# First block of a retention and two-MoE kernel: fourteen weight subtractions and five scalings from VectorE to GpSimd, three state scalings from ScalarE to VectorE

## The chip, the cores and the metric

The kernel runs on 1 core of one Trainium2 chip. The metric is device time in microseconds (us) for one execution; the text uses the median of several runs, and one more execution was profiled. The engines named are PE (TensorE: matrix products; PEld is its weight load), DVE (VectorE), ACT (ScalarE), POOL (GpSimd) and SP (SyncE, which here only issues DMAs). Each engine works through its own instructions strictly in their order; semaphores make it wait for the others.

## The reference

```python
# retention, per batch (4) and head (8), 768 steps, head size 64
state = gamma * state + outer(k[t], v[t]);  y[t] = scale * q[t] @ state
x = y as 3072 tokens x 512
# first feed-forward
h = x @ w_in                 # 512 -> 2048
g = maximum(0.01 * h, h)
x = g @ w_out                # 2048 -> 512
# then a mixture of 8 experts, top 1, 512 -> 1024 -> 512, scaled by two gates
```

The change touches the retention and the weights `w_in` and `w_out` of the first feed-forward. These two arrays come in as 64-bit floats.

## The kernel before

The 3072 tokens are worked through in 8 blocks of 384 (`TB`), and a block is 3 chunks of 128 tokens. A chunk is one step of the retention, which is done chunk by chunk: chunks 0 to 2 make block 0, and while block i goes through the feed-forward, the three chunks of block i+1 are computed between its products. Behind the 8 blocks lie routing and the experts, which the change doesn't touch.

**The loop of a block.** Each block runs 16 steps, f = 0 to 15, over 128 of the 2048 hidden columns each. Step f has `mm1` (12 matmuls of 128x384, line L307), then `act` and `act_b`, and `mm2` of the step before (9 matmuls of 128x512, L348), which adds to the three output banks. Every operand is split into a high part, which TensorE multiplies quickly, and a low part, which is the rest; a product is low times high, high times low and high times high. So behind `mm1` comes a chain: ACT scales h by 0.01 (`t`, L325), DVE takes the maximum (`t`, L326), ACT rounds to the high part (`gh`, L328), DVE subtracts for the low part (`gl`, L335). `mm2` begins with `gl`.

**Preparing the weights.** Block 0 also has to bring the 64-bit weights into high and low parts, one piece of 128x512 of `w_in` and one of `w_out` (index 0 and 1) per step. `conv` does it with the letters A and D (ACT, L151 and L157), B and C (DVE, L159 and L164), H (ACT, L176: high part) and L (L178: low part = value minus high part). In step f of block 0 the DVE's order is: `t`, L of the next `w_in` piece, `gl`, L of the next `w_out` piece, then B twice and C twice for the pieces after. `mm2` of step f uses the low part of `w_out` piece f one to two steps after it was made. The raw pieces are loaded by SP through a ring of four pairs of buffers; a load waits until L has read the pair that it overwrites. The constant `LOP` lists the pieces whose L goes to GpSimd; it is empty before.

**The retention chunk.** In step f = 3, 7 and 11 of block 0 the scores of chunks 3, 4 and 5 are made (`attn_a`, PE L229), and DVE multiplies them by a mask (`am`, L235, twice 128x512). In steps 5, 9 and 13 follows `attn_b`: the outputs `y` (L263, L265), the update of the state `U` (L244), the high and low parts of x (`xh` ACT L274, `xl` DVE L275), then `attn_state` (the state bank is copied to SBUF with a scale for each head, tile `sbd`), `attn_q` and `attn_k` (q and k are scaled in place by tables, L213 and L219). The first set of these three, for chunk 3, stands in step 1. Chunks from 6 on have their q and k scaled by GpSimd and their state by VectorE already.

The line that chooses the engine of L is in `conv_op`; n is the piece, x is 0 for `w_in` and 1 for `w_out`:

```python
(nc.gpsimd if (n, x) in LOP else nc.vector).tensor_sub(lo, val, hi.bitcast(F32))
```

Of the kernel before, what the change touches and what calls it, by code (L numbers as in the profile page):

```python
# [14 lines left out]
ACTF = mybir.ActivationFunctionType  # L15
# [17 lines left out]
FS = [1, 0, 2, 0, 0, 1]  # L33
NSLOT = 2 * NP + NS
XW = 516
LOP = ()
LOWV = ()
AHEAD_S = [(p, c) for p in range(2) for c in range(4)]
AHEAD_P = [(p, 2 * g + c) for g in range(2) for p in range(2) for c in range(2)]
# [18 lines left out]
def tile_retention_moe_moe(  # L58
# [12 lines left out]
    nc = tc.nc  # L71
# [12 lines left out]
    kd = mq[:, :48].rearrange("p (c g) -> p c g", c=6)  # L84
    sc = mq[:, 48:72].rearrange("p (c j) -> p c j", c=6)
    past = mq[:, 72:200]
    qd = mq[:, 200:712]
# [50 lines left out]
    def conv_op(o, n, m, x, f):  # L138
# [27 lines left out]
        if o in "HL":  # L166
# [10 lines left out]
            else:  # L177
                (nc.gpsimd if (n, x) in LOP else nc.vector).tensor_sub(lo, val, hi.bitcast(F32))  # L178

# [7 lines left out]
    sbd = [const.tile([128, 4, 128], F32, name="sbd")]  # L187
    n_b = [0]
    U = {}
# [20 lines left out]

    def attn_q(n):
        q = loads[n][0]
        (nc.vector if n in (0, 2, 3, 4, 5) else nc.gpsimd).tensor_mul(q, q, qd)  # L213

    def attn_k(n):
        cc = n % (2 * NC)
        if cc < 5:
            k = loads[n][2].rearrange("p (g d) -> p g d", d=64)
            (nc.vector if n in (2, 3, 4) else nc.gpsimd).tensor_mul(k, k, kd[:, cc].unsqueeze(2).to_broadcast([128, 8, 64]))  # L219

    def pairs():
        return [(j, h, slice(64 * h, 64 * h + 64), slice(j * 128 + 64 * h, j * 128 + 64 * h + 64), slice(j * 128, (j + 1) * 128))
# [23 lines left out]
    def attn_state(n):  # L246

        b, cc = divmod(n, 2 * NC)
        for h in range(2):
            r = slice(64 * h, 64 * h + 64)  # L250
            if 2 < n < 6:
                for j in range(4):
                    nc.scalar.activation(out=sbd[0][r, j, r], in_=U[b][r, j, r], func=ACTF.Copy, scale=sc[r, cc, j:j + 1])
                continue
            nc.vector.tensor_mul(sbd[n % 2 if n < 3 else 0][r, :, r], U[b][r, :, r], sc[r, cc].unsqueeze(2).to_broadcast([64, 4, 64]))

    def attn_y(n, am, tag="m0"):
# [27 lines left out]
    def attn_b(n, am):  # L285
        y = attn_y(n, am)
        if n % 6 < 5:
            attn_U(n)
        attn_x(n, y)
        if n % 6 < 5:  # L290
            attn_state(n + 1)
        attn_next(n)
        if n + 1 < NB * NC:
            attn_q(n + 1)
            attn_k(n + 1)
# [430 lines left out]
    for x in ORDER:  # L726
        k = sum(y[0] == x for y in items)
# [302 lines left out]
    with tc.manual_schedule():  # L1030
# [20 lines left out]
        def keep_warm(n):  # L1051
            for _ in range(n):
                nc.tensor.matmul(warm[:, :256], sbd[0][:, 0], sbd[0].rearrange("p j c -> p (j c)")[:, :256], start=True, stop=True)

        attn_k(0)
        attn_q(1)
        attn_k(1)
        banks = attn_scores(0, ("m0", "m1"))
        keep_warm(KW[0])
# [6 lines left out]
        banks = attn_scores(1, ("x20", "x21"))  # L1066
        keep_warm(KW[2])
        attn_state(1)
        conv("L", -1)

# [6 lines left out]
        attn_next(0)  # L1077
        y = attn_y(1, am1, "x20")
        attn_state(2)
        attn_q(2)  # L1080
        banks = attn_scores(2, ("x22", "h1"))
        keep_warm(KW[3])
# [175 lines left out]
```

## Time and profile before

| | |
|---|---|
| median of 3 runs | 1012.31 us (1010.25 to 1012.48) |
| profiled execution | 1009.34 us, its span 1007.5 us |
| PE busy | 981.7 us (97%) |
| DVE busy | 561.5 us (56%) |
| ACT busy | 447.1 us (44%) |
| POOL busy | 196.4 us (19%) |
| mean granted TensorE clock | 0.995 |

The span is the time from the first to the last instruction in the trace. The shares are means over very different stages: the preparing of weights lies between about 26 and 107 us, the blocks without it follow up to about 650 us, the experts come last. Granted clock 1.00 is TensorE's higher level of 2.4 GHz, 0.50 the lower of 1.2 GHz.

### The profile page before, as it was taken

The page shows a single profiled execution, that of the slowest core. Times are in us where ns is not written, and L with a number is a line of the kernel's source. Part 1 is how long each engine was busy: PE and PEld are TensorE (multiplying, and loading weights), DVE is VectorE, ACT ScalarE, POOL GpSimd, SP SyncE. Part 2 cuts the span into 40 slices and gives each one's busy share as a digit, 9 for nine tenths or more (in the row PEclk, how much of TensorE's full clock was granted, in tenths as well). Part 3 has the DMA queues.
Part 4 walks back from the last instruction along what each step waited for, and adds up shares of the span by engine and source line. Part 5 has one row for each costly group of instructions (what it writes and reads, how often), then busy time and mean ns, then how long its engine had stood idle before and what let it go on. Part 6 is the DMA issues. An engine that isn't in the chain of part 4 may idle for free.

```text
span 1007.5 us, 16953 instructions
## 1 busy us (share of the span) xinstructions
PE 981.7 (97%) x6525; PEld 870.8 (86%) x6525; DVE 561.5 (56%) x1087; ACT 447.1 (44%) x791; POOL 196.4 (19%) x148
## 2 busy tenths in 40 slices
PE   7899999999999999999999999999999999999996
PEld 5787888888889888988989898888888988888995
DVE  5899543534344444443444367465648657666762
ACT  3888332223222222232222233435548667665752
POOL 2001021021012011011110001623323333333122
PEclk9999999999999999999999999999999999999998
DMA  9674222322322222214303004002139779776511
GB/s 365 228 236 150 83 58 59 89 59 58 90 59 58 60 78 69 59 51 98 58 32 74 17 32 168 21 33 75 42 122 310 265 250 318 277 247 216 191 43 35
DMA packets 75366, 121.64 MB, mean 121 GB/s; under 512 B 36238, under 2 KB 36622, under 8 KB 72464
## 3 DMA queue, kind: packets, MB, share of 16 engines
q1 hardware_dynamic: 70352, 105.96, 34.1%
q0 software_dynamic: 4640, 14.18, 4.1%
q8 instruction: 53, 0.87, 0.4%
q10 hardware_dynamic: 288, 0.36, 0.2%
q14 instruction: 33, 0.27, 0.1%
HBM read 125.97 MB, written 13.64 MB: 139 GB/s over the span
## 4 chain that ended last, share of the span: by engine, by line
PE 85%; DVE 7%; ACT 3%; issue 2%; DMA 1%; POOL 1%; another core or an unknown queue 0%; SPq 0%; POOLq 0%; DVEq 0%
PE x L348 24%; PE h L307 24%; PE m L847 10%; PE m L872 10%; PE m L897 3%; PE m L925 3%; PE ay L229 2%; PE y L265 2%; PE y L263 2%; PE xt L816 1%; DVE raw L159 1%; DMA kv<-in_qkv_dram 1%; DVE wl L178 1%; PE u L244 1%; PE lg L476 1%
## 5 line engine op out<-in xcount | busy, mean ns | idle before, releaser
L783 DVE TENSOR_TENSOR wu<-raw,wu 128x1024 fp32r<-128x1024 f32 x114 | 148.9, 1337 | 58.8 <-ACT wu L782 56.5
L326 DVE TENSOR_TENSOR t<-t,h 128x384 f32<-128x384 f32 x127 | 70.1, 552 | 134.6 <-ACT t L325 134.5
L847 PE MATMUL m<-xe,wu 128*128 128x256 f32 x1056 | 137.5, 284 | 0.8 <-DVE gl L859 0.8
L782 ACT CAST wu<-raw 128x1024 fp32r<-128x1024 f32 x136 | 137.2, 1048 | 1.6 <-DMA raw<-in_w_dram 1.4
L325 ACT ACTIVATE t<-h 128x384 f32<-128x384 f32 x127 | 62.2, 490 | 169.7 <-PE h L307 139.9
L847 PEld LDWEIGHTS m<-xe,wu 128*128 128x128 f32 x1056 | 132.4, 191 | 3.7 <-DVE gl L859 1.0
L335 DVE TENSOR_TENSOR gl<-t,gh 128x384 fp32r<-128x384 f32 x127 | 80.5, 634 | 90.9 <-ACT gh L328 90.9
L328 ACT CAST gh<-t 128x384 fp32r<-128x384 f32 x127 | 65.3, 514 | 128.8 <-PE x L348 68.7
L348 PE MATMUL x<-wh,gl 128*128 128x512 f32 x288 | 116.1, 403 | 6.2 <-DVE gl L335 6.2
L348 PE MATMUL x<-wl,gh 128*128 128x512 f32 x288 | 113.9, 395 | 0.0
L348 PE MATMUL x<-wh,gh 128*128 128x512 f32 x288 | 113.5, 394 | 0.0
L872 PE MATMUL m<-wu,gh 128*128 128x512 f32 x352 | 109.1, 391 | 0.0
L455 POOL TENSOR_TENSOR xr<-xr,b 128x512 f32<-128x512 f32 x18 | 21.0, 1165 | 405.0 <-DVE gl L335 241.0
L307 PE MATMUL h<-xh,wl 128*128 128x384 f32 x384 | 85.3, 343 | 0.0
L307 PE MATMUL h<-xl,wh 128*128 128x384 f32 x384 | 82.6, 336 | 0.0
L783 POOL TENSOR_TENSOR wu<-raw,wu 128x1024 fp32r<-128x1024 f32 x22 | 55.5, 2531 | 137.8 <-ACT wu L782 131.0
L307 PE MATMUL h<-xh,wh 128*128 128x384 f32 x384 | 82.1, 334 | 0.0
L872 PEld LDWEIGHTS m<-wu,gh 128*128 128x128 f32 x352 | 66.3, 188 | 12.5
L348 PEld LDWEIGHTS x<-wh,gl 128*128 128x128 f32 x288 | 54.3, 189 | 21.3 <-DVE gl L335 8.8
L872 PE MATMUL m<-wu,gl 128*128 128x512 f32 x176 | 69.8, 396 | 1.2 <-DVE gl L859 0.9
L307 PEld LDWEIGHTS h<-xh,wl 128*128 128x128 f32 x384 | 67.1, 188 | 3.8
L307 PEld LDWEIGHTS h<-xl,wh 128*128 128x128 f32 x384 | 69.0, 188 | 0.0
(232 smaller groups left out, 1519.8 us busy)
## 6 DMA issues: line engine op xcount, KB each, us to landing
raw<-in_w_dram SPq DMA_DIRECT2D x175, 512.0 KB
kv<-in_qkv_dram SPq DMA_DIRECT2D x22, 1024.0 KB
x2d<-xr SPq DMA_DIRECT2D x24, 256.0 KB
kv<-in_qkv_dram SPq DMA_DIRECT2D x4, 512.0 KB
t<-b SPq DMA_TRANSPOSE x36
stg<-in_w_dram SPq DMA_DIRECT2D x1, 512.0 KB
kv<-x2d,gidx POOLq DMA_INDIRECT x18
mq<-in_cm_dram ACTq DMA_DIRECT2D x1, 256.0 KB
```

The source lines that it names most:

```text
L307: nc.tensor.matmul(h, wcols(a, fc * 512 + k * 128, 128), x[:, k, :], start=(n == 0), stop=(n == 11))
L325: nc.scalar.activation(out=t, in_=h, func=ACTF.Copy, scale=0.01)
L326: nc.vector.tensor_max(g, t, h)
L328: nc.scalar.copy(out=ghi, in_=g)
L335: nc.vector.tensor_sub(glo, g, ghi.bitcast(F32))
L348: nc.tensor.matmul(x2ps[i][t], a[:, ts], wcols(w, f % 4 * 512), start=(f == 0 and n == 0), stop=(f == 15 and n == 2))
L782: nc.scalar.copy(out=hi, in_=src)
L783: (nc.gpsimd if g == 0 or (p, c) in POOL_LO[g >= NP] else nc.vector).tensor_sub(lo, src, hi.bitcast(F32))
L847: nc.tensor.matmul(bank, wp_[k // 2][a][:, c:c + 128], x[:, k, :], start=(n == 0), stop=(n == 11))
L872: nc.tensor.matmul(m2ps[2 * q + h], a[:, ts], w[:, fs], start=(f == 0 and n == 0), stop=(f == 7 and n == 2))
L897: nc.tensor.matmul(buf["b"], a[:, kk], w[:, k0:k0 + 512], start=(k == 0 and n == 0), stop=(k == 3 and n == 2))
L925: nc.tensor.matmul(m2ps[s], a[:, kk], w[:, f0:f0 + 512], start=(k == 0 and n == 0), stop=(k == 7 and n == 2))
```

## The change

The low parts (L) of the `w_out` pieces 1 to 14 are made by GpSimd; those of `w_in` and of piece 0 and 15 stay with VectorE. q of chunks 3, 4 and 5 and k of chunks 3 and 4 are scaled by GpSimd (k of chunk 5 needs no scaling). The states of chunks 3 to 5 are scaled by VectorE in two instructions of 64x256, in place of eight of 64x64 on ScalarE.

```diff
-LOP = ()
+LOP = [(n, 1) for n in range(1, 15)]
...
     def attn_q(n):
         q = loads[n][0]
-        (nc.vector if n in (0, 2, 3, 4, 5) else nc.gpsimd).tensor_mul(q, q, qd)
+        (nc.vector if n in (0, 2) else nc.gpsimd).tensor_mul(q, q, qd)
 
     def attn_k(n):
         cc = n % (2 * NC)
         if cc < 5:
             k = loads[n][2].rearrange("p (g d) -> p g d", d=64)
-            (nc.vector if n in (2, 3, 4) else nc.gpsimd).tensor_mul(k, k, kd[:, cc].unsqueeze(2).to_broadcast([128, 8, 64]))
+            (nc.vector if n == 2 else nc.gpsimd).tensor_mul(k, k, kd[:, cc].unsqueeze(2).to_broadcast([128, 8, 64]))
...
         for h in range(2):
             r = slice(64 * h, 64 * h + 64)
-            if 2 < n < 6:
-                for j in range(4):
-                    nc.scalar.activation(out=sbd[0][r, j, r], in_=U[b][r, j, r], func=ACTF.Copy, scale=sc[r, cc, j:j + 1])
-                continue
             nc.vector.tensor_mul(sbd[n % 2 if n < 3 else 0][r, :, r], U[b][r, :, r], sc[r, cc].unsqueeze(2).to_broadcast([64, 4, 64]))
```

Since the diff takes four lines out, lines from L254 on stand four lower in the changed kernel: `gl` is L331 there, the maximum L322, `xl` L271, the state on VectorE L251.

VectorE, from the `gl` of step 4 to the maximum of step 6 of the first block, before:

```order
L335 TENSOR_TENSOR gl<-t,gh 128x384
L178 TENSOR_TENSOR wl_493<-raw,wh_491 128x512
L159 SCALAR_TENSOR_TENSOR raw<-raw 128x512 x2
L164 SCALAR_TENSOR_TENSOR raw<-raw 128x512 x2
L275 TENSOR_TENSOR xl<-y,xh 128x4x128
L213 TENSOR_TENSOR kv<-kv,mq 128x512
L219 TENSOR_TENSOR kv<-kv,mq 128x512
L326 TENSOR_TENSOR t<-t,h 128x384
```

The same place of VectorE's queue in the changed kernel:

```order
L331 TENSOR_TENSOR gl<-t,gh 128x384
L159 SCALAR_TENSOR_TENSOR raw<-raw 128x512 x2
L164 SCALAR_TENSOR_TENSOR raw<-raw 128x512 x2
L271 TENSOR_TENSOR xl<-y,xh 128x4x128
L251 TENSOR_TENSOR sbd<-u,mq 64x4x64 x2
L322 TENSOR_TENSOR t<-t,h 128x384
```

The subtraction behind `gl` and the two scalings behind `xl` have left, and two instructions on the state bank have come.

GpSimd's queue before, from the scaling of k of chunk 1 to the first instruction of the second block's routing:

```order
L219 TENSOR_TENSOR kv<-kv,mq 128x512
L213 TENSOR_TENSOR kv<-kv,mq 128x512
L219 TENSOR_TENSOR kv<-kv,mq 128x512
L455 TENSOR_TENSOR xr<-xr,b_1306 128x512
```

The same part in the changed kernel, up to the seventh subtraction (the other seven, the q of chunk 5 and the scalings of chunk 6 follow in the same manner):

```order
L219 TENSOR_TENSOR kv<-kv,mq 128x512
L178 TENSOR_TENSOR wl_277<-raw,wh_275 128x512
L178 TENSOR_TENSOR wl_278<-raw,wh_276 128x512
L213 TENSOR_TENSOR kv<-kv,mq 128x512
L219 TENSOR_TENSOR kv<-kv,mq 128x512
L178 TENSOR_TENSOR wl_278<-raw,wh_276 128x512
L178 TENSOR_TENSOR wl_486<-raw,wh_484 128x512 x2
L178 TENSOR_TENSOR wl_487<-raw,wh_485 128x512
L213 TENSOR_TENSOR kv<-kv,mq 128x512
L219 TENSOR_TENSOR kv<-kv,mq 128x512
L178 TENSOR_TENSOR wl_487<-raw,wh_485 128x512
```

GpSimd, which had nothing there but the scalings of chunk 6, now has a subtraction in each step, and in steps 1 and 5 two scalings right behind it.

ScalarE in step 1 of the first block, before:

```order
L157 ACTIVATE raw<-raw 128x512 x2
L253 ACTIVATE sbd<-u,mq 64x64 x8
L325 ACTIVATE t<-h 128x384
```

and in the changed kernel, where the eight small instructions ahead of `t` are gone:

```order
L157 ACTIVATE raw<-raw 128x512 x2
L321 ACTIVATE t<-h 128x384
```

## Rows read from the trace of the kernel before

**Rows 1.** The page, busy time, share of the span and instructions of each engine.

```profile
PE 981.7 (97%) x6525; PEld 870.8 (86%) x6525; DVE 561.5 (56%) x1087; ACT 447.1 (44%) x791; POOL 196.4 (19%) x148
```

**Rows 2.** Windows: length, busy PE, PEld, DVE, ACT, POOL, clock, DMA share, GB/s.

```profile
36.00:99.00 63.00, 58.20 (x376) 49.74 (x376) 61.57 (x105) 55.93 (x118) 2.75 (x2) 0.97 0.58 194
...
38.00:40.00 2.00, 2.00 (x6) 1.59 (x5) 2.00 (x4) 2.00 (x5) 0.00 (x0) 0.50 0.76 260
40.00:42.00 2.00, 2.00 (x8) 1.62 (x8) 1.92 (x4) 1.96 (x9) 0.00 (x0) 0.65 0.71 229
```

**Rows 3.** Waits of 26 to 107 us (total, times, longest), then PE's timeline.

```profile
PE x L348 <- DVE gl L335: 5.5, 8, 2.1
...
37.67 0.55 PE L348 MATMUL x<-wh,gl 128*128 128x512 f32 x1 [2.12 <-DVE gl L335]
```

**Rows 4.** Chain that ended last, one step of block 0: start, us, what.

```profile
49.75 0.60 DVE wl L178
50.35 1.21 DVE raw L159 x2
51.56 1.20 DVE raw L164 x2
...
53.14 0.69 DVE wl L178
53.83 0.53 DVE gl L335
```

**Rows 5.** Timeline of DVE in step 0: start, us, instruction, idle before it.

```profile
32.71 1.30 DVE L159 SCALAR_TENSOR_TENSOR raw<-raw 128x512 uint32<-128x512 uint32 x2 [0.98 <-ACT raw L157]
```

**Rows 6.** Groups by line: 36 to 99 us (busy, mean ns), then whole span (ns min/median/max).

```profile
L253 ACT ACTIVATE sbd<-u,mq 64x64 f32<-64x64 f32 x24 | 5.4, 300 | 0.0
...
L783 POOL TENSOR_TENSOR wu<-raw,wu x22: 2385/2407/3202, 625.2 to 990.9; 128x1024 fp32r<-128x1024 f32 x22
...
L213 POOL TENSOR_TENSOR kv<-kv,mq x19: 1269/1292/1307, 11.5 to 540.3; 128x512 f32<-128x512 f32 x19
...
L219 POOL TENSOR_TENSOR kv<-kv,mq x17: 1042/1048/1496, 7.7 to 525.9; 128x512 f32<-128x512 f32 x17
```

**Rows 7.** Timeline of DVE, state scaling of chunk 2.

```profile
15.81 0.85 DVE L255 TENSOR_TENSOR sbd<-u,mq 64x256 f32<-64x256 f32 x2
```

**Rows 8.** Timelines of POOL and DVE at two places where both work.

```profile
90.74 1.30 POOL L213 TENSOR_TENSOR kv<-kv,mq 128x512 f32<-128x512 f32 x1 [76.53 <-DMA kv<-in_qkv_dram]
92.00 1.49 POOL L219 TENSOR_TENSOR kv<-kv,mq 128x512 f32<-128x512 f32 x1
...
90.75 0.54 DVE L326 TENSOR_TENSOR t<-t,h 128x384 f32<-128x384 f32 x1
91.21 1.38 DVE L178 TENSOR_TENSOR w<-val,w 128x512 fp32r<-128x512 f32 x1
...
132.26 1.05 POOL L219 TENSOR_TENSOR kv<-kv,mq 128x512 f32<-128x512 f32 x1
...
132.37 1.35 DVE L335 TENSOR_TENSOR gl<-t,gh 128x384 fp32r<-128x384 f32 x1 [1.32 <-ACT gh L328]
```

**Rows 9.** Timelines of POOL and DVE, two large POOL subtractions back to back.

```profile
625.16 4.76 POOL L783 TENSOR_TENSOR wu<-raw,wu 128x1024 fp32r<-128x1024 f32 x2 [68.84 <-ACT wu L782]
...
625.33 2.27 DVE L611 TENSOR_SCALAR rt<-rt 128x2 f32<-128x2 f32 x1
627.63 2.32 DVE L612 CAST gidx<-rt 128x2 int32<-128x2 f32 x1
```

**Rows 10.** Timelines of ACT and DVE, step 3 of block 0, with the mask.

```profile
47.94 0.66 ACT L176 CAST wh<-raw 128x512 fp32r<-128x512 f32 x1
...
49.20 0.55 DVE L335 TENSOR_TENSOR gl<-t,gh 128x384 fp32r<-128x384 f32 x1
```

**Rows 11.** Timelines of DVE and PE, step 13: low part, and its product.

```profile
102.97 0.56 DVE L335 TENSOR_TENSOR gl<-t,gh 128x384 fp32r<-128x384 f32 x1
...
105.28 0.39 PE L348 MATMUL x<-w,gl 128*128 128x512 f32 x1
```

## The prediction

> **What bounds the kernel now.** I read the busy times first: over the whole span PE is busy 97% [rows 1], so nothing outside PE's queue can matter unless PE waits for it. The second view is the list of waits, stretch by stretch. In the preparing of weights, 26 to 107 us, PE waits eight times for `gl`, 5.5 us in all; the longest, 2.12 us, comes at 37.67 [rows 3]. The third is the windows: from 36 to 99 us DVE is busy 61.57 of 63.0 us, 98%, ACT 55.93, PE 58.20, POOL 2.75 [rows 2]. So there DVE and PE are both nearly full, and it is DVE that PE waits for. The fourth is the chain that ended last: a plain step of block 0 runs along DVE alone, L of `w_out` 0.60, B 1.21, C 1.20, the maximum, L of `w_in` 0.69, `gl` 0.53, from 49.75 to the next L at 54.36, 4.61 us [rows 4]. What the change is worth is thus read on DVE: a microsecond taken from its queue between 36 and 99 us shortens the block only until PE's waits are gone; a microsecond added lengthens it in full, since DVE has 63.0 - 61.57 = 1.43 us idle in all.
>
> **What leaves and what comes on VectorE.** I count up to the `gl` of step 12, because behind it DVE has room: the `gl` of step 13 ends at 102.97 + 0.56 = 103.53 and its product starts at 105.28, 1.75 us later [rows 11]. The L of piece 1, in step 0, is worth nothing, since DVE idles 0.98 us for ACT right behind it [rows 5]. The L of pieces 2 to 12 are 11 instructions of 0.60 us in the chain [rows 4]: 6.6 us. The five scalings of q and k are of the same shape and I take the same 0.60: 3.0 us. The three states come back as two instructions of 0.85 us together [rows 7]: 2.55 us. DVE's queue thus gets shorter by 6.6 + 3.0 - 2.55 = 7.05 us.
>
> ACT loses 24 instructions, 5.4 us [rows 6]. ACT isn't the fuller engine; where its eight small ones held up `t`, DVE idled, and that is within the 1.43 us that I count below. Alone this is worth nothing more.
>
> **What GpSimd does to VectorE.** The price of the moved work is not POOL's time, it has plenty. Look at the two places where both engines work [rows 8]. At 91.21 DVE begins an L that takes 1.38 us instead of 0.69; POOL's q scaling ends at 92.04 and DVE's L at 92.59, 0.55 us after it. POOL's next, k, takes 1.49 us instead of its usual 1.05 [rows 6] and ends 0.90 us after DVE's L. At 132.37 a `gl` takes 1.35 us instead of 0.55 and ends 0.41 us after POOL's k at 133.31. But the maximum at 90.75, which has one input in PSUM, takes its usual 0.54 beside POOL. So an instruction of DVE with both inputs in SBUF and an instruction of POOL exclude each other: the later one stands until the earlier one is done, and then needs 0.14 us less than alone (0.69 to 0.55, 0.55 to 0.41). L, B, C and `gl` are of that kind, some 3.7 of the 4.61 us of a step. The maximum, the mask, `xl` and the state read PSUM and are not.
>
> The Trainium skill (SBUF — State Buffer, "Who interferes with whom") says the same and more strictly: VectorE with two SBUF inputs and a GpSimd instruction that reads SBUF share one port pair, the first to start holds it for its whole instruction, the other is blocked fully. By that rule, with no 0.14 us off, the sum below would end at +8.2 us instead of +6.1; the trace agrees but for these 0.14 us.
>
> Now the new instructions of POOL. L on POOL isn't in this trace at this size; the same subtraction at twice the width has a median of 2.41 us [rows 6], half is 1.20, less 0.14 is 1.06 us of standstill for DVE. From below the price is 0.5 (under the rivals), from above the whole 1.20. I take 1.06 because of when it comes: POOL can start when H on ACT ends, H follows `gh`, and `gl` on DVE follows `gh` too, so POOL asks just when DVE starts B, and B and C are 2.4 us of the exclusive kind. The eight L of steps without a mask cost 8 x 1.06 = 8.5 us. In steps 3, 7 and 11 the mask stands ahead of `gl`: H ends at 48.60, POOL would work to 49.8 and `gl` end at 50.2 instead of 49.75 [rows 10], so 0.5 each, 1.5 us. Three q of 1.29 - 0.14 = 1.15 make 3.45, two k of 0.90 make 1.8; they stand right behind an L in POOL's queue, and so fall between the other B and C of that step. Sum of the standstills: 15.25 us.
>
> **Sum.** -7.05 + 15.25 = +8.2 us. Off go DVE's 1.43 us of idle time and the 0.69 us that the L at 91.21 stands for POOL now: the scalings of chunk 6 come behind piece 14 in the changed queue, beyond step 12. That leaves +6.1 us. The pieces 13 and 14 fall into the 1.75 us of room; with the scalings of chunk 6 they could exceed it by 1.2 us, which I keep for the upper end. The profiled execution of 1009.34 us would become 1015.4. It lies 3 us under the median of 1012.31, and the runs are compared by medians: 1018.4 us.
>
> **Costed at nothing.** PE needs the low parts of `w_out` one step or more after they are asked for, about 5 us, and POOL needs 1.20, or 3.5 with two scalings ahead, plus up to 0.6 for each wait on DVE. If that cover went, PE would stand at the second matmul of `mm2`. The scores need q two steps after its scaling. SP's loads of raw pieces wait for POOL's reading instead of DVE's, one or two us later; the list of waits from 36 us on has no ACT instruction that waits for such a load, and a piece is used two steps, some 9 us, after its load is issued. What stands behind a DVE instruction that waits for POOL is everything: the maximum and `gl`, and behind them PE.
>
> **Rivals.** *GpSimd waits for the gaps.* The trace shows POOL and DVE taking turns: two large subtractions of POOL back to back, and DVE's L611 slips in between them after 2.27 us, L612 only after the second, 2.32 us [rows 9]. It doesn't show POOL asking while DVE has several exclusive instructions in a row. If DVE keeps its way until it turns to PSUM, POOL's work lies beside the maximum (0.46 us from its start to the next one's [rows 8]) or the mask, and beside `xl` (0.6), state (0.85) and maximum in steps 5 and 9. A plain L then costs 1.06 - 0.46 = 0.60, five of them 3.0; the masks 1.5; step 1 with both scalings 3.1 - 1.3 = 1.8, step 5 3.1 - 1.9 = 1.2, step 9 2.2 - 1.9 = 0.3: 7.8 us. Then -7.05 + 7.8 - 2.12 = -1.4 us, 1010.9. It decides at the price of a plain L: the forecast turns into no gain near 0.5 us each.
>
> *Pure relief.* If POOL cost DVE nothing, DVE would fall under PE, and PE's waits of 5.5 us would go but for the 2.12 us at 37.67, where ACT is late in step 0 with work that stays: -3.4 us, 1008.9. Rows 8 speak against it.
>
> *Full locks and a slower clock.* With whole instructions (8 x 1.20 + 3 x 0.6 + 3 x 1.29 + 2 x 1.05 = 17.4) the sum is +8.2, with the tail +9.4. And behind the wait of 2.12 us PE fell to a granted clock of 0.50 (the 1.2 GHz level) in 38 to 40 us and 0.65 in the next two [rows 2], which lost 0.5 x 2 + 0.35 x 2 = 1.7 us. Steps 1 and 5, with three standstills, can make such a wait again: +11.1, 1023.4. Against it: the mean clock of 0.97 over 36 to 99 us is used up by this one fall (1.7 of 63 us), so PE's shorter waits there had none behind them, and a slow PE hides partly while DVE is behind.
>
> *Half hidden.* If DVE waits elsewhere when POOL works more often than I count, +2 us, 1014.3.
>
> **How the numbers follow.** A change of 0.3%, 3.0 us, is about what a measurement of this kernel can tell. Chances: the forecast 0.54, with its own range of 1015.5 to 1021.5; gaps 0.21; relief 0.07; locks and clock 0.13; half hidden 0.05. Slower by over 0.3%: 0.54 + 0.13 = 0.67. Within: 0.21 + 0.05 less 0.02 for gaps that come out better, 0.24. Faster: 0.07 + 0.02 = 0.09. The range leaves out relief, a little of the gaps below, and the upper half of locks and clock: 1009.8 to 1022.8.
>
> **What would show it.** In the changed profile L178 on POOL at about 1.2 us or up to 1.8 with its wait, thirteen of them between DVE's B and C; B, C, L or `gl` of 1.2 to 1.7 us instead of 0.55 to 0.69 once or more in each step of block 0; plain steps of about 5.1 us instead of 4.6; PE's waits for `gl` grown from 5.5 to some 11 us or more; everything behind block 0 unchanged but shifted by about 6 us. I am wrong if DVE's B and C keep 0.69 us beside POOL, if POOL's rows stretch to 3 us (the gaps), or if the block ends no later than before.

## The result and the profile after

The changed kernel takes 1017.58 us (median of 6 runs, 1016.68 to 1019.35), the kernel before 1012.17 us (6 runs, 1010.25 to 1012.59): a ratio of 1.0058, 95% interval 1.0045 to 1.0070, so 5.9 us slower (the ratio is taken over all runs; the two medians lie 5.4 us apart). The profiled execution is the shortest of the six, 1016.68 us with a span of 1014.9.

First DVE's timeline of the changed kernel: the plain step 4 to 5, then the mask of step 3 with the `gl` behind it, then B and C of step 5, where the two scalings follow the subtraction on GpSimd (start, us, instruction, count; the two in a "x2" are one piece).

```profile
57.45 0.56 DVE L331 TENSOR_TENSOR gl<-t,gh 128x384 fp32r<-128x384 f32 x1
57.93 2.42 DVE L159 SCALAR_TENSOR_TENSOR raw<-raw 128x512 uint32<-128x512 uint32 x2
60.28 1.28 DVE L164 SCALAR_TENSOR_TENSOR raw<-raw 128x512 uint32<-128x512 uint32 x2
...
62.60 0.56 DVE L331 TENSOR_TENSOR gl<-t,gh 128x384 fp32r<-128x384 f32 x1
...
51.62 1.28 DVE L235 TENSOR_TENSOR am<-ay,mq 128x512 f32<-128x512 f32 x2
52.82 1.18 DVE L331 TENSOR_TENSOR gl<-t,gh 128x384 fp32r<-128x384 f32 x1
...
63.07 2.43 DVE L159 SCALAR_TENSOR_TENSOR raw<-raw 128x512 uint32<-128x512 uint32 x2
65.43 3.25 DVE L164 SCALAR_TENSOR_TENSOR raw<-raw 128x512 uint32<-128x512 uint32 x2
```

And GpSimd's timeline of the same steps:

```profile
52.28 1.31 POOL L178 TENSOR_TENSOR wl<-raw,wh 128x512 fp32r<-128x512 f32 x1 [3.40 <-ACT wh L176]
58.06 1.74 POOL L178 TENSOR_TENSOR wl<-raw,wh 128x512 fp32r<-128x512 f32 x1 [4.48 <-DVE gl L331]
...
63.21 1.74 POOL L178 TENSOR_TENSOR wl<-raw,wh 128x512 fp32r<-128x512 f32 x1 [3.41 <-ACT wh L176]
64.92 1.77 POOL L213 TENSOR_TENSOR kv<-kv,mq 128x512 f32<-128x512 f32 x1
66.63 1.50 POOL L219 TENSOR_TENSOR kv<-kv,mq 128x512 f32<-128x512 f32 x1
```

Read them together. At 58.06 GpSimd asks while DVE's first B runs; it stands until that B is over, about 58.62, and works to 59.80. The second B, which would have begun at 58.54, ends at 60.35. So the pair takes 2.42 us instead of 1.29: one subtraction on GpSimd costs DVE 1.13 us. Beside the mask GpSimd needs 1.31 us unhindered, and the `gl` behind it 1.18 instead of 0.56: 0.62 us. In step 5 the subtraction costs 1.14 (2.43) and the two scalings 1.96 together (3.25 instead of 1.29). The plain step from 57.45 to 62.60 is 5.15 us long. Before, the same step took 4.72 us, from 53.80 to 58.52:

```profile
53.68 0.66 ACT L176 CAST wh<-raw 128x512 fp32r<-128x512 f32 x1
53.80 0.56 DVE L335 TENSOR_TENSOR gl<-t,gh 128x384 fp32r<-128x384 f32 x1
54.36 0.69 DVE L178 TENSOR_TENSOR wl<-raw,wh 128x512 fp32r<-128x512 f32 x1
54.97 1.29 DVE L159 SCALAR_TENSOR_TENSOR raw<-raw 128x512 uint32<-128x512 uint32 x2
...
58.52 0.56 DVE L335 TENSOR_TENSOR gl<-t,gh 128x384 fp32r<-128x384 f32 x1
```

From `gl` to B it was 1.17 us, since L had to wait until ScalarE's high part ended at 54.34; now it is 0.48. So the L that left was worth 0.69 us here: by these prices the step loses 1.13 - 0.69 = 0.44 us, and it is 0.43 longer.

The waits of PE from 26 to 115 us, as a total, and its longest ones in its own timeline:

```profile
PE x L344 <- DVE gl L331: 12.3, 8, 2.5
...
39.18 0.55 PE L344 MATMUL x<-wh,gl 128*128 128x512 f32 x1 [2.11 <-DVE gl L331]
54.05 0.50 PE L344 MATMUL x<-wh,gl 128*128 128x512 f32 x1 [2.46 <-DVE gl L331]
78.72 0.50 PE L344 MATMUL x<-wh,gl 128*128 128x512 f32 x1 [2.46 <-DVE gl L331]
102.49 0.50 PE L344 MATMUL x<-wh,gl 128*128 128x512 f32 x1 [2.45 <-DVE gl L331]
```

12.3 us for 5.5 before [rows 3], and the wait behind ACT at 39.18 is the same 2.11. The windows from 36 to 105 us show DVE still full and POOL now at work (columns as in [rows 2]); the two short ones show the clock ahead of everything that the change moves:

```profile
36.00:105.00 69.00, 56.93 (x372) 48.95 (x371) 68.18 (x94) 50.99 (x94) 25.85 (x16) 0.98 0.55 183
...
26.00:28.00 2.00, 2.00 (x19) 1.88 (x20) 1.93 (x4) 0.59 (x2) 0.00 (x0) 0.50 1.01 404
28.00:30.00 2.00, 2.00 (x10) 2.00 (x10) 0.57 (x1) 0.00 (x0) 0.00 (x0) 0.69 1.06 420
```

In this execution TensorE fell to its 1.2 GHz level at 26 us (0.50, then 0.69), which lost about 1.7 us; in the profiled execution of before the same windows have a clock of 1.00. PE had just waited 3.21 us for k of chunk 2 in both. Such falls also come where the programs are the same: e_hold below differs from before only behind 90 us and has two of them ahead of 32 us. To compare profiles without them I read one stretch on DVE, **from the start of the `gl` of step 1 to the start of the `gl` of step 12**. It is 61.25 us before (37.06 to 98.31) and 67.31 after (38.57 to 105.88): +6.06 us. The other 1.5 us between the two profiles lie ahead of step 0's `gl`, before any work that the change moves, and fit the fall at 26 us.

### The profile page after: what moved, and what is told of

It is laid out like the page before. It is cut to its first block, busy times and chain, and to the rows that moved or that the text cites. A ratio compares the mean times of both kernels' runs of the same rounds, so it can differ in the third digit from the quotient of the medians.

```text
span 1014.9 us, 16985 instructions
## 1 busy us (share of the span) xinstructions
PE 981.9 (97%) x6525; PEld 871.8 (86%) x6525; DVE 568.9 (56%) x1074; ACT 441.6 (44%) x767; POOL 225.8 (22%) x167
## 4 chain that ended last, share of the span: by engine, by line
PE 85%; DVE 9%; issue 2%; DMA 1%; ACT 1%; POOL 1%; another core or an unknown queue 0%; SPq 0%; POOLq 0%; DVEq 0%
PE x L344 24%; PE h L303 24%; PE m L843 11%; PE m L868 10%; PE m L893 3%; PE m L921 3%; DVE raw L159 2%; PE ay L229 2%; PE y L261 2%; PE y L259 2%; DVE raw L164 1%; PE xt L812 1%; DMA kv<-in_qkv_dram 1%; PE u L244 1%; PE lg L472 1%
## 5 line engine op out<-in xcount | busy, mean ns | idle before, releaser
L322 DVE TENSOR_TENSOR t<-t,h 128x384 f32<-128x384 f32 x127 | 70.0, 551 | 134.3 <-ACT t L321 134.2
L331 DVE TENSOR_TENSOR gl<-t,gh 128x384 fp32r<-128x384 f32 x127 | 83.2, 655 | 90.9 <-ACT gh L324 90.9
```

The source lines that it names most:

```text
L322: nc.vector.tensor_max(g, t, h)
L331: nc.vector.tensor_sub(glo, g, ghi.bitcast(F32))
```

## The experiments

Theory: GpSimd's reading instructions and DVE's two-input instructions exclude each other in turns, and DVE is the full engine. Rivals: GpSimd gets in only where DVE turns to PSUM; or not the exclusion but later low parts, the states, or the clock. The runs, with that stretch and the ratio of times to before:

| run | `gl` 1 | `gl` 12 | stretch | against before | ratio, 95% interval |
|---|---|---|---|---|---|
| before | 37.06 | 98.31 | 61.25 | | |
| the change | 38.57 | 105.88 | 67.31 | +6.06 | 1.0058 (1.0045 to 1.0070) |
| e_low | 38.77 | 101.96 | 63.19 | +1.94 | 1.0025 (1.0015 to 1.0035) |
| e_qk | 44.60 | 106.41 | 61.81 | +0.56 | 1.0032 (1.0019 to 1.0044) |
| e_state | 38.20 | 100.66 | 62.46 | +1.21 | 1.0025 (1.0015 to 1.0036) |
| e_qk_state | 40.42 | 99.86 | 59.44 | -1.81 | 1.0007 (0.9993 to 1.0021) |
| e_low_state | 37.08 | 102.69 | 65.61 | +4.36 | 1.0050 (1.0036 to 1.0064) |
| e_low_qk | 38.46 | 103.06 | 64.60 | +3.35 | 1.0037 (1.0023 to 1.0051) |
| e_twice | 40.77 | 110.92 | 70.15 | +8.90 | 1.0130 (1.0115 to 1.0145) |
| e_write | 40.10 | 100.73 | 60.63 | -0.62 | 1.0043 (1.0029 to 1.0056) |
| e_odd | 41.55 | 104.45 | 62.90 | +1.65 | 1.0022 (1.0010 to 1.0034) |
| e_hold | 39.75 | 100.34 | 60.59 | -0.66 | 0.9988 (0.9979 to 0.9996) |

**The subtractions alone.** `LOP` as in the change, the rest as before:

```diff
-LOP = ()
+LOP = [(n, 1) for n in range(1, 15)]
```

> Only the 14 subtractions go to GpSimd; q, k and the states stay where they were. If GpSimd's reads and VectorE's two-input instructions exclude each other (theory), VectorE loses 11 x 0.60 = 6.6 us of work up to step 12 and stands still for 8 x 1.13 + 3 x 0.6 = 10.8 us (the stretched rows of the changed kernel): +4.2, less 0.7 for the chunk 6 scalings that come later and 0 to 1.4 us of idle time: +2.1 to +3.5 us against before, most of the whole change. If moving work off VectorE is relief and only the states on VectorE or a slower TensorE clock cost (rival): 0 to -3 us.

+1.94 us in the stretch, 1.0025 in time (2.5 us): close under the theory's band, clear of the rival's.

**q and k alone.** The two lines of `attn_q` and `attn_k` as in the change.

```diff
-        (nc.vector if n in (0, 2, 3, 4, 5) else nc.gpsimd).tensor_mul(q, q, qd)
+        (nc.vector if n in (0, 2) else nc.gpsimd).tensor_mul(q, q, qd)
...
-            (nc.vector if n in (2, 3, 4) else nc.gpsimd).tensor_mul(
+            (nc.vector if n == 2 else nc.gpsimd).tensor_mul(
```

> Only q and k of chunks 3 to 5 go to GpSimd, whose queue is otherwise empty there, so that they can run as soon as chunk and buffers are there and need not fall between B and C. Theory: VectorE loses 3.0 us of work; what it stands still depends on where they fall, at most 2 x 2.05 + 1.15 = 5.3 us: -2 to +1 us. Rival (each instruction given to GpSimd costs about half a microsecond net wherever it falls): +2 us.

Missed: 1.0032, about +3.2 us, and hardly any of it in the stretch (+0.56). GpSimd's timeline of this run, then DVE's and PE's:

```profile
24.86 1.49 POOL L213 TENSOR_TENSOR kv<-kv,mq 128x512 f32<-128x512 f32 x1 [10.74 <-DMA kv<-in_qkv_dram]
26.32 1.03 POOL L219 TENSOR_TENSOR kv<-kv,mq 128x512 f32<-128x512 f32 x1
27.38 1.66 POOL L213 TENSOR_TENSOR kv<-kv,mq 128x512 f32<-128x512 f32 x1
29.00 1.49 POOL L219 TENSOR_TENSOR kv<-kv,mq 128x512 f32<-128x512 f32 x1
...
26.73 2.86 DVE L178 TENSOR_TENSOR wl<-raw,wh 128x512 fp32r<-128x512 f32 x2
29.51 1.52 DVE L219 TENSOR_TENSOR kv<-kv,mq 128x512 f32<-128x512 f32 x1
...
31.09 1.12 PE L244 MATMUL u<-kv 128*64 128x64 f32 x16 [5.64 <-DVE kv L219]
```

With nothing ahead of them in the queue, four scalings run as soon as chunk 3 has landed, at 24.86, and meet DVE where it prepares step 0: L twice 2.86 us, k of chunk 2 1.52 us, and PE waits 5.64 us for that k instead of 3.2. I had taken "early" for free, and early was a time when PE waited directly behind DVE. Behind that wait TensorE ran at or near its 1.2 GHz level from 28 to 36 us (a granted clock of 0.83, then 0.50 in three windows of 2 us). The twelve runs of this kernel form two groups: five of 1011.31 to 1013.04 us with a mean clock of 0.994 to 0.996, and seven of 1014.99 to 1017.85 us with 0.988 to 0.991. The profiled one is the longest. So most of the 3.2 us goes with the clock; that the longer wait makes such falls more frequent was not shown. In the change the subtractions stand ahead of the scalings in GpSimd's queue and hold them back to steps 1 and 5.

**The states alone,** the four ScalarE lines of `attn_state` taken out:

```diff
-            if 2 < n < 6:
-                for j in range(4):
-                    nc.scalar.activation(out=sbd[0][r, j, r], in_=U[b][r, j, r], func=ACTF.Copy, scale=sc[r, cc, j:j + 1])
-                continue
```

> Only the three states go from ScalarE to VectorE. Theory (VectorE is the full engine): +2.55 us on VectorE less its 1.4 us of idle time, which ScalarE caused: 0 to +1.5 us. Rival (the small ScalarE instructions hold the block up): -1.5 us or more, since ScalarE loses 5.4 us.

+1.21 us in the stretch, as the theory has it; in time 1.0025, 2.5 us, more than it; where the other 1.3 us lie was not traced. ScalarE's 5.4 us less bring no gain.

**q, k and states, without the subtractions** (the last two diffs together):

> q, k and states moved as in the change, the 14 subtractions left on VectorE. Theory: VectorE's queue shrinks by 3.0 - 2.55 = 0.45 us and ScalarE's waits go; with GpSimd's scalings early: -2 to +1 us against before, 5 to 7 us faster than the change. Rival (the subtractions are not what costs): as slow as the change, +5 us.

1.0007, no difference that can be told, and -1.81 us in the stretch: with q, k and states moved but the subtractions left, the block itself gets shorter, and what it gains is lost ahead of it: the `gl` of step 1 starts 3.4 us later than before (PE waits 4.3 us for k of chunk 2, and the granted clock is 0.50 from 26 to 32 us).

**The pairs with the subtractions** (the first diff with the third, and with the second):

> Subtractions and states moved, q and k left on VectorE. I read the stretch from the gl of step 1 to the gl of step 12, which leaves out what the clock does ahead of it: 61.25 us before, 67.31 us with the whole change. Theory (the ledger of VectorE with the measured prices 1.13 and 0.62): -6.6 + 2.55 + 8 x 1.13 + 3 x 0.62 - 0.7 - 1.4 = +4.7 us. Rival (the single edits add up, 1.94 + 1.21 from their own runs): +3.2 us.

+4.36 us, between the two but nearer to the ledger's 4.7 than to the 3.2 of plain adding.

> Subtractions, q and k moved, the states left on ScalarE. The scalings stand behind the subtractions in GpSimd's queue and so fall between B and C of steps 1 and 5, not into the time ahead of step 0 as when they moved alone. Theory, same stretch: -9.6 + 10.9 + 2 x 1.96 + 1.1 - 0.7 = +5.6 us, less 0 to 1.4 of idle time: +4.2 to +5.6. Rival (single edits add up, 1.94 + 0.56): +2.5 us.

+3.35 us, between the ledger's band from 4.2 and the rival's 2.5: no decision. With the states on ScalarE, part of the standstill lies beside DVE's waits for ScalarE. Counted from `gl` to `gl`, steps 1, 5 and 9 come out 0.5, 0.4 and 0.9 us below the ledger, 1.8 us in all, where I had taken off at most 1.4. The rest is that the removed L were worth more than 6.6 us (below).

**The subtractions twice.** DVE makes all of them as before, GpSimd makes them again into a scratch tile:

```diff
                 (nc.gpsimd if (n, x) in LOP else nc.vector).tensor_sub(lo, val, hi.bitcast(F32))
+                if x == 1 and 0 < n < 15:
+                    nc.gpsimd.tensor_sub(scr, val, hi.bitcast(F32))
...
+    scr = gp.tile([128, XW], F32R, tag="xs", bufs=1, name="scr")[:, :512]
```

> VectorE makes all low parts as before; GpSimd makes those of pieces 1 to 14 a second time into a scratch tile that nobody reads. No work is taken from VectorE and none is waited for. Theory (the two engines exclude each other, by turns): VectorE stands 8 x 1.13 + 3 x 0.6 = 10.9 us up to step 12, less 0.7 for the chunk 6 scalings that come later and up to 1.4 us of idle time: +8.8 to +10.2 us. Rival one (GpSimd only gets in where VectorE turns to PSUM): 8 x 0.6 + 1.8 = 6.6, +4.5 to +6 us. Rival two (no such thing; the cost of the change was the later low parts or the states): 0.

+8.90 us in the stretch: the theory of turns, against 4.5 to 6 and 0 of the rivals. One plain step, GpSimd and DVE:

```profile
60.71 1.79 POOL L180 TENSOR_TENSOR scr<-raw,wh 128x512 fp32r<-128x512 f32 x1 [5.13 <-DVE gl L338]
...
60.61 0.69 DVE L178 TENSOR_TENSOR wl<-raw,wh 128x512 fp32r<-128x512 f32 x1
61.22 2.43 DVE L159 SCALAR_TENSOR_TENSOR raw<-raw 128x512 uint32<-128x512 uint32 x2
```

Nobody waits for what GpSimd makes here, and the standstill is the same (2.43 for 1.29, 1.14 us). That shows the mutual exclusion as the cause, without the moved work.

**Writing only.** In place of the second subtraction GpSimd fills the scratch tile twice, started by a fill of one column on VectorE:

```diff
+                if x == 1 and 0 < n < 15:
+                    nc.vector.memset(scr[:, 0:1], 0.0)
+                    nc.gpsimd.memset(scr, 0.0)
+                    nc.gpsimd.memset(scr, 1.0)
...
+    scr = gp.tile([128, XW], F32, tag="xs", bufs=1, name="scr")[:, :512]
```

> As before, and in the same fourteen places GpSimd fills the scratch tile with a constant twice (2 x 0.53 us), started by a fill of one column on VectorE. GpSimd writes SBUF and reads nothing. Theory (it is GpSimd's reading that excludes two-input instructions of VectorE): VectorE's B and C keep 0.69 us; only the small fills cost, 11 x 0.06 to 0.1 us: 0 to +1 us. Rival (any work of GpSimd in SBUF does it): +6 to +10 us.

```profile
58.16 0.53 POOL L181 MEMSET scr<- 128x512 f32 x1 [3.60 <-DVE scr L180]
58.76 0.53 POOL L182 MEMSET scr<- 128x512 f32 x1
...
58.01 0.69 DVE L159 SCALAR_TENSOR_TENSOR raw<-raw 128x512 uint32<-128x512 uint32 x1
58.03 0.06 DVE L180 MEMSET scr<- 128x1 f32 x1
58.61 0.69 DVE L159 SCALAR_TENSOR_TENSOR raw<-raw 128x512 uint32<-128x512 uint32 x1
```

GpSimd works nearly as long in the same place (1.13 us from the first start to the second end), and B keeps 0.69 us; the stretch is 0.62 us shorter (the scalings of chunk 6 fall behind step 12 here). So work of GpSimd that only writes SBUF does not do it. What the fills leave out is the reading; a GpSimd instruction that reads in another way than these subtractions and scalings was not tried. The time, 1.0043, is outside what was expected, and another matter: in this run and in e_twice the scratch tile takes a buffer of the later routing, and from the first store of block 0 to that of block 7 it is 545.3 us here (118.51 to 663.82) and 545.6 in e_twice, instead of 541.7 before (115.99 to 657.66). Why these blocks are 3.6 us longer wasn't traced; it is not in block 0.

**Six of the subtractions,** in plain steps:

```diff
-LOP = ()
+LOP = [(n, 1) for n in range(3, 15, 2)]
```

> Only pieces 3, 5, 7, 9, 11 and 13 go to GpSimd, all in steps without a mask. Theory of turns: 5 x (1.13 - 0.60) = +2.7 up to step 12, less 0.7 for chunk 6 and up to 1.4 idle: +0.6 to +2.0 us, GpSimd's L rows 1.7 us. Rival (GpSimd waits until VectorE turns to PSUM, as a scaling of chunk 6 did for 4.4 us in the runs with VectorE's queue unbroken): -0.7 to 0 us, L rows of 3 us and more.

+1.65 us, inside the theory's band, GpSimd's rows 1.73 to 1.89 us: turns.

**One subtraction, to hold the scalings of chunk 6 back:**

```diff
-LOP = ()
+LOP = [(14, 1)]
```

> As before, with the L of piece 14 alone on GpSimd: it stands in the tail where VectorE has 1.75 us of room, and it keeps the two scalings of chunk 6, behind it in GpSimd's queue, from falling into step 10. Theory: the 0.69 us standstill at 91 us goes and nothing comes: -0.7 us, 0 to -1 in time. Rival (work on GpSimd there costs the same anywhere): 0 to +0.5 us.

-0.66 us in the stretch, ratio 0.9988 (0.9979 to 0.9996): 1.2 us faster than before, the only version here that beats both kernels.

**A form of scaling.** In e_qk, e_qk_state and e_state the k scaling of chunk 6 takes 4.4 us on GpSimd. From e_state, GpSimd and DVE:

```profile
95.76 4.43 POOL L219 TENSOR_TENSOR kv<-kv,mq 128x512 f32<-128x512 f32 x1
...
95.73 0.55 DVE L331 TENSOR_TENSOR gl<-t,gh 128x384 fp32r<-128x384 f32 x1
96.19 0.68 DVE L178 TENSOR_TENSOR w<-val,w 128x512 fp32r<-128x512 f32 x1
96.79 1.29 DVE L159 SCALAR_TENSOR_TENSOR raw<-raw 128x512 uint32<-128x512 uint32 x2
98.00 1.29 DVE L164 SCALAR_TENSOR_TENSOR val<-raw 128x512 uint32<-128x512 uint32 x2
99.20 0.55 DVE L322 TENSOR_TENSOR t<-t,h 128x384 f32<-128x384 f32 x1
99.67 1.07 DVE L178 TENSOR_TENSOR w<-val,w 128x512 fp32r<-128x512 f32 x1
```

DVE goes through six exclusive instructions at their usual length while GpSimd stands, and gives way only at the maximum, 99.20: the way of the rival that I had given 0.21. On top of e_state:

```diff
+            if n == 6:
+                nc.gpsimd.tensor_mul(loads[n][2], loads[n][2], qd)
+                return
```

> States on VectorE as in the run of the states alone, and k of chunk 6 is scaled with the plain table of q in place of its own broadcast one (chunk 6 comes out otherwise; its time is what counts). There k's scaling asked at the start of the gl of step 11 and stood 3.4 us through gl, L, B, B, C, C. If the broadcast form is what lets VectorE keep its way: now about 1.3 to 1.8 us. If it is the place: 4.4 us again.

In a single execution the scaling took 1.62 us and the L behind the `gl` 1.79: turns again. That speaks for the broadcast form, but GpSimd also asked 0.16 us after the `gl` had started, not 0.03, and that `gl` had just stood for GpSimd. Nor is it the form alone: in the changed kernel the same broadcast form took its turn at 66.63 (1.50 us). What lets DVE keep its way stays open.

## Why the prediction was right

It said 1018.4 us, +6.1; measured are 1017.58 and +5.9 by the ratio (4.6 to 7.1), +6.06 in the stretch that its sum was made for. The mechanism held. That the sum came within 0.1 us is partly luck, since three of its terms were off and cancelled, as the next points show.

- *DVE bounds this part.* Right: 68.18 of 69 us busy after, and the waits of PE for `gl` grew from 5.5 to 12.3 us ("some 11 or more").
- *The standstills.* Right in kind, a little small in size: a plain L 1.13 us (forecast 1.06), one beside the mask 0.62 (0.5), two scalings 1.96 (2.05). With these prices they come to 8 x 1.13 + 3 x 0.62 + 2 x 1.96 + 1.11 (C of step 9, 2.39 instead of 1.28) = 15.9 us for 15.25.
- *What left, and the idle time.* Both sized too small, and they make up for it. The eleven L that left were worth 7.1 us, not 6.6. In steps 1, 4, 5, 8 and 9 the L had waited for ScalarE's high part, and `gl` to B took 1.16 to 1.20 us before and 0.47 or 0.48 after; in the other six steps the L was worth the 0.60 of the forecast. What is left, 1.6 us where 1.43 us of idle time was taken off, lies in steps 1, 5 and 9, those with ScalarE's state scalings before. The other eight steps fit these prices within 0.02 us: from `gl` to `gl`, steps 2 and 6 are 0.53 and 0.54 us longer (1.13 - 0.60), steps 4 and 8 0.43 and 0.44, the three with a mask 0.01 to 0.03 (0.62 - 0.60), and step 10 is 0.19 shorter. The prediction also counts 3.7 of the 4.61 us of a step as exclusive; both L, B, C and `gl` of [rows 4] add up to 4.2. No term used it.
- *The states.* 2.55 us forecast on DVE; the change minus e_low_qk is 67.31 - 64.60 = 2.71 us. And ScalarE's relief was worth no more than DVE's idle time.
- *The 0.69 us of chunk 6.* e_hold takes just that away: 0.66 us.
- *Turns, not gaps.* Right for all thirteen L up to the end of block 0 that DVE's work met (rows of 1.27 to 1.76 us); the gaps do exist, as e_state shows, so the chance for them was no idle one.
- *The clock.* The fall that I priced at 1.7 us did not come more often inside the block (36 to 105 us: 0.98) in the profiled execution, where one more came ahead of it, at 26 us. That execution has the highest mean clock of the six, 0.994; the others have 0.989 to 0.992. And behind waits of PE like those at 54.05 and 102.49 TensorE did fall to its 1.2 GHz level in other runs with the subtractions moved: at 52 to 58 us in e_low, e_low_state and e_low_qk, at 98 to 104 us in the last two. From e_low, where PE had waited 1.82 us until 52.67 (columns as in [rows 2]):

```profile
52.00:54.00 2.00, 1.33 (x4) 1.12 (x5) 2.00 (x4) 1.45 (x3) 0.20 (x1) 0.81 0.83 266
54.00:56.00 2.00, 2.00 (x6) 1.57 (x5) 2.00 (x4) 1.18 (x3) 0.00 (x0) 0.50 0.51 201
```

  Beside a full DVE that fall cost nothing: steps 3 and 4 take 4.63 and 5.14 us there and 4.63 and 5.15 in the changed kernel at a clock of 1.00. At the end of block 0 it came with a loss: from the `gl` of step 12 to the block's first store it is 19.4 us in e_low_state and e_low_qk, 17.9 in the change and in e_low, which have no fall there. So the rival's clock was not idle, and how often it fell in the five executions without a profile is not known. Why the profiled execution of before lay 3 us under its median was not shown; falls of 1.7 us are of that size.
- *The tail.* Pieces 13, 14 and chunk 6 cost 0.2 us of the 1.2 feared: PE's list has no wait behind 102.49, and the 17.9 us to the first store were 17.7 before.

## What to carry to other kernels

Before work goes from VectorE to GpSimd, count which VectorE instructions beside it read two operands from SBUF: here each 128x512 subtraction took 0.60 to 0.72 us off VectorE and made it stand 1.13 us, so that an engine that idles 95% cost the full one more than it gave. Beside the mask, which reads PSUM, it gave and cost about the same (0.60 and 0.62); in the steps where VectorE had idled for ScalarE it cost next to nothing (e_low, steps 1, 5 and 9: 0.00 to 0.07 us longer). An in-order queue in front of such work decides when it falls there: one subtraction placed late held two scalings out of the full stretch and made the kernel 1.2 us faster. Where executions differ by clock falls outside the part that is changed, compare a stretch between two marks on the bounding engine, not the spans.

## What the runs showed of the hardware

- GpSimd's 128x512 subtraction with two SBUF inputs takes 1.27 to 1.33 us beside the mask, where nothing holds it up; asked for in the middle of VectorE's exclusive instructions, 1.70 to 1.89, let in at the next boundary in every run here. Fills of 0.53 us that read nothing disturb none of these instructions.
- The same VectorE queue can also keep a GpSimd instruction out: 4.43 to 4.47 us for a k scaling of 1.04 us, in three kernels at the same place. I found no rule that covers both.
- TensorE fell to its 1.2 GHz level in one to four places of each profiled execution, between 12 and 104 us, and lost 1.7 us or twice that in each; the places differ in executions of nearly the same program. The runs of before alone span 1008.36 to 1013.38 us.
